# Moving weight conversions and gate products in a fused attention and channel-mixing kernel

## The chip, the cores and the metric

One core of one Trainium2 chip runs the whole program. The metric is device time in microseconds (us) of one execution. Three executions of the kernel before took 931.25 us in the median (930.16 to 931.75).

## The reference

The program computes three layers, all in float32. The first is attention with pooled queries; its output, laid out as x of shape (4, 576, 512), goes through a gated channel mixture, and that through a mixture over tokens and channels:

```
xk = mu_k * x + (1 - mu_k) * x_prev          # x_prev: x one token earlier
xr = mu_r * x + (1 - mu_r) * x_prev
k = max(xk @ w_k, 0)                         # 512 -> 1024
v = k * k @ w_v                              # 1024 -> 512
x = sigmoid(xr @ w_r) * v
theta = x @ w_theta
y = w_tok_r @ (x * cos(theta)) + w_tok_i @ (x * sin(theta))
u = x + y
out = u + max(u @ w_ch, 0)
```

The weights come as float64. The kernel turns each into a pair of float32r numbers, a high part and the rest, and every product of matrices is made of three matmuls (high by high, high by low, low by high).

## The kernel before, in words

**Stages.** Attention takes the first 427 us or so. The gated mixture follows until about 719 us, then the token mixture to the end. The gated mixture works on eight blocks of 288 tokens. Each block i needs three steps on TensorE (PE):

- `gate(i)` (L803): 48 matmuls, xr by w_r into four PSUM banks. ACT makes the sigmoid of them (L816).
- `hidden(i)` (L834): 96 matmuls, xk by w_k, eight groups f of 12. For each f ACT takes the ReLU (L836), DVE squares it (L837), ACT copies the high part (L820) and POOL subtracts for the low part (L821).
- `value(i)` (L853): 96 matmuls, the squares by w_v, eight f of 12, into four banks. At the end DVE makes four **gate products** (L858), bank by sigmoid, into the tile `XT`. They free the four banks.

PE takes them in the order gate 0, 1, 2, hidden 0, gate 3, value 0, hidden 1, gate 4, value 1, and so on, one block ahead with three gates.

**The inputs of a step.** For hidden(i) and gate(i) four input pairs x are made, one for each 128 channels: ACT scales (`xmul`, L771), DVE adds the other token (`xadd`, L776), ACT copies the high part (L782), and DVE or POOL subtracts for the low part (L783). `ahead` does this in one go for hidden(0), behind gate(1)'s matmuls.

**Ticks.** All engines read their instructions in the order in which they are written. Work beside the matmuls is hung on a counter: `tick()` is called after each f of hidden and value and after each quarter of a gate, and emits what `queue` holds for that number. Gate(1) has ticks 10 to 13, gate(2) 14 to 17, hidden(0) 18 to 25, gate(3) 26 to 29, value(0) 30 to 37, hidden(1) 38 to 45; value(5) has 126 to 133, hidden(6) 134 to 141.

**Two kinds of conversion run beside the gated mixture.**

- Five *late pieces* of w_v (k = 3 to 7, `late_v`). Their float64 words are loaded at the end of attention (L946). Each takes three ticks: first ACT's absolute value (L959) and POOL's clamp (L960); then three bit operations on DVE (L962 to L964); then ACT's high part (L967) and POOL's low part (L968). The tick of the first step is `LATE_TICK + LATE_PACE * (k - early_v)`, that is 14, 16, 18, 20, 22.
- 43 *conversion jobs* of the second mixture's weights (`conv_steps`), one every 2.7 ticks: ACT's absolute value (L127), four DVE operations (L130 to L142), ACT's copy (L146), POOL's subtraction (L150) and two stores by SP (L154, L155). The constant `SHIFT` puts all but the first load so many ticks later. The first job's DVE operations are at tick 20, the last job's at tick 133.

Loads and stores all go through SP's queue. In the second mixture `theta` (L1075) is the first user of converted weights, which SP loads with L1007.

Of the kernel before, what the change touches and what calls it, by code (L numbers as in the profile page):

```python
# [29 lines left out]
WARM = 16  # L30
THIRDS = 6
AHEAD = 3
SHIFT = 16
TURN = 4
TPOS = ((1, 0), (1, 3), (2, 0), (3, 0), (3, 3))
THETA = (1, 2, 4, 5)
# [11 lines left out]

PIECES = {"a": ((1, 2), ((2, 2), (2, 2), (2, 2)), (9, 2), 14, 15), "x": ((1, 2), ((2, 2), (2, 2), (2, 2)), (3, 2), 5, 7)}
LATE = 5  # L50
LATE_TICK = 14
LATE_PACE = 2

F64_MIN = float(np.array([0x38000000], np.uint32).view(np.float32)[0])
F64_MAX = float(np.array([0x47EFFFFF], np.uint32).view(np.float32)[0])
# [8 lines left out]
def attn_moe_kernel(ctx: ExitStack, tc: tile.TileContext, qT, kT, vP, muk, mur, wk, wv, wr, wth, wtr, wti, wch, ident, out):  # L64
# [94 lines left out]
    def attention(first):  # L159
# [491 lines left out]

        at(NT - 2, load_wr)
        follow = mixtures(WR, nat, cp)
        first_x = next(follow)
        for s, step in zip((NT - 9, NT - 7, NT - 4, NT - 2), first_x):
# [49 lines left out]
    def mixtures(WR, nat, cp):  # L705
# [9 lines left out]
        def psum():  # L715
            nb[0] += 1
            if late:
                return psum_at(LB[nb[0] % len(LB)])
            return (psm if not psn else (psm + psn))[(nb[0] - 1) % (6 if not psn else 8)]()
# [33 lines left out]
        queue = {}  # L753
# [4 lines left out]
        def tick():  # L758
            now[0] += 1
            for fn, args in queue.pop(now[0], []):  # L760
                fn(*args)
# [84 lines left out]
        def value(i, inner=()):  # L846
            b, c0 = work[i]
            k2, sg = k2s.pop(i), sgs.pop(i)
            pss = [psum()[:, :HALF] for d in range(4)]
            for f in range(8):  # L850
                for d in range(4):
                    for n, (w, c) in enumerate(PASS):
                        pe.matmul(pss[d], lhsT=WV[f][:, w, 128 * d:128 * d + 128], rhs=k2[f][:, c], start=(f == 0 and n == 0), stop=(f == 7 and n == 2))  # L853
                tick()
                if f in inner:
                    inner[f]()
            for d in range(4):
                dve.tensor_tensor(XT[b][:, d, c0:c0 + HALF], pss[d], sg[d], ALU.mult)  # L858
            if c0 and b % 2:
                pool.tensor_scalar(XT[b - 1][:, :, 576:640], XT[b][:, :, 512:576], 1.0, 1.0, op0=ALU.mult, op1=ALU.mult)  # L860

# [51 lines left out]
        for i, piece in enumerate(jobs):  # L913
            for o, f in zip((-2, 2, 3, 3, 3, 3, 4, 4, 5), conv_steps(room, piece, i, pool)):
                if o == 0 and i < 1:
                    f()
                else:
                    queue.setdefault(int(t) + o + SHIFT, []).append((f, ()))
            t += PACE
# [21 lines left out]
        early_v = 8 - LATE  # L941
# [27 lines left out]

        for k in range(early_v, 8):  # L970
            for step in range(3):
                queue.setdefault(LATE_TICK + LATE_PACE * (k - early_v) + step, []).append((late_v, (k, step)))
        order = [(gate, 0), (gate, 1), (gate, 2)]
        for i in range(8):
            order.append((hidden, i))
            if i + AHEAD < 8:
                order.append((gate, i + AHEAD))
            order.append((value, i))
# [180 lines left out]
        hidden(6)  # L1159
        theta(0)  # L1160
        value(6)
        theta(1)
        hidden(7)
        theta(2)
        value(7, {3: lambda: theta(3)})
        theta(4)
        WTK = [tile_b(8)] + [None] * 8
# [69 lines left out]
```

## Time and profile before

| | |
|---|---|
| median of three runs | 931.25 us |
| the profiled execution's own time | 932.49 us |
| its span in the trace | 930.5 us |
| PE busy | 907.8 us, 98% of the span |
| DVE, POOL, ACT busy | 74%, 64%, 58% |
| waits of PE for gate products from 500 to 760 us | 4.8 us, the longest 3.3 us |

The span covers the instructions; the execution's own time is 2 us longer. PE is almost always busy, so the places of interest are the few stretches in which it stands or runs at the lower clock. Times of single instructions are read from the trace with their start in microseconds of the span.

### The profile page before, as it was taken

Reading aid. Unit: us, or ns where it says so; the run is one execution under the profiler, and the core shown is the slowest. Engines: PE = TensorE matmul, PEld = TensorE weight load, DVE = VectorE, ACT = ScalarE, POOL = GpSimd, SP = SyncE. Lnnn points to the kernel's source line nnn. Section 1 sums busy time; section 2 is a strip of 40 time slices with the busy share of each in tenths; the row PEclk is TensorE's granted clock in tenths of the full one; section 3 lists DMA queues with packets and bytes.
Section 4 is the critical chain, followed back from the end, with each engine's and each line's share of the span. In section 5 each row is a group of like instructions: output and inputs, shape, how many; then the busy total and the mean of one; then the engine's idle time right before and its main releaser. Section 6 shows DMA issues by size and latency. Waiting matters only on the chain.

```text
span 930.5 us, 17357 instructions
## 1 busy us (share of the span) xinstructions
PE 907.8 (98%) x6292; PEld 786.4 (85%) x6292; DVE 686.7 (74%) x965; ACT 541.9 (58%) x1133; POOL 594.2 (64%) x662
## 2 busy tenths in 40 slices
PE   8999999999999999999889999998999999999998
PEld 6677777777777777768888999998999999999998
DVE  7888888888898888872699888888347663676712
ACT  8777777777777777764645565555344343443310
POOL 7877777777788777763466565666347574674631
PEclk9999999999999999999989999999899999999999
DMA  7268886777777776669323323233206200010001
GB/s 242 86 176 227 237 225 187 218 211 207 217 213 210 209 235 186 186 183 365 137 70 112 103 86 103 86 119 124 107 1 213 82 27 27 1 51 2 26 26 51
DMA packets 58773, 129.74 MB, mean 139 GB/s; under 512 B 10752, under 2 KB 29888, under 8 KB 58688
## 3 DMA queue, kind: packets, MB, share of 16 engines
q1 hardware_dynamic: 58688, 128.64, 46.4%
q8 instruction: 49, 0.80, 0.4%
q14 instruction: 36, 0.29, 0.1%
HBM read 70.46 MB, written 22.17 MB: 100 GB/s over the span
## 4 chain that ended last, share of the span: by engine, by line
PE 83%; DVE 8%; ACT 4%; issue 3%; POOL 1%; DMA 0%; SPq 0%; ACTq 0%; DVEq 0%; POOLq 0%
PE sc L303 18%; PE ty L423 16%; PE ps L1129 12%; PE ps L834 7%; PE ps L853 7%; PE ps L1148 5%; PE ps L1075 5%; PE ty L389 4%; PE tx L389 3%; PE ps L803 2%; PE sc L389 2%; DVE a L134 1%; DVE a L138 1%; ACT e L336 1%; PE ps L1033 1%
## 5 line engine op out<-in xcount | busy, mean ns | idle before, releaser
L324 DVE TENSOR_REDUCE m<-sc 128x1 f32<-128x1152 f32 x138 | 185.8, 1346 | 48.5 <-PE sc L303 47.8
L336 ACT ACTIVATE e<-sc,m 128x1152 f32<-128x1152 f32 x144 | 176.4, 1225 | 60.8 <-DVE m L324 56.2
L303 PE MATMUL sc<-kt,q 128*128 128x384 f32 (+1 forms) x864 | 192.7, 351 | 3.1 <-ACT M L400 1.7
L303 PEld LDWEIGHTS sc<-kt,q 128*128 128x128 f32 (+1 forms) x864 | 146.7, 190 | 24.4 <-issue 13.6
L834 PE MATMUL ps<-x,a 128*128 128x288 f32 x768 | 107.3, 300 | 5.8 <-DVE xt L858 4.8
L1129 PE MATMUL ps<-b,a 128*128 128x288 f32 x816 | 111.3, 296 | 0.0
L834 PEld LDWEIGHTS ps<-x,a 128*128 128x128 f32 x768 | 105.1, 193 | 6.8 <-DVE xt L858 5.5
L1129 PEld LDWEIGHTS ps<-b,a 128*128 128x128 f32 x816 | 109.4, 188 | 0.6
L853 PE MATMUL ps<-k,b 128*128 128x288 f32 x768 | 103.8, 295 | 0.1
L853 PEld LDWEIGHTS ps<-k,b 128*128 128x128 f32 x768 | 102.1, 188 | 0.6 <-ACT h L836 0.4
L202 POOL TENSOR_TENSOR kt<-kn,kh 64x576 fp32r<-64x576 f32 (+1 forms) x64 | 87.5, 1387 | 2.4
L356 DVE STREAM_TRANSPOSE blk<-e 128x1152 f32<-128x1152 f32 x60 | 81.6, 1360 | 7.4 <-ACT e L336 7.4
L423 PE MATMUL ty<-M,vn 128*64 128x320 f32 x576 | 84.4, 438 | 0.2 <-ACT M L400 0.2
L423 PEld LDWEIGHTS ty<-M,vn 128*64 128x64 f32 x576 | 38.7, 136 | 36.3 <-issue 3.8
L469 POOL TENSOR_TENSOR xt<-xt,rb 128x576 f32<-128x576 f32 x16 | 21.9, 1371 | 73.0 <-ACT xt L433 73.0
L821 POOL TENSOR_TENSOR k<-h,k 128x288 fp32r<-128x288 f32 x64 | 56.4, 897 | 18.1 <-ACT k L820 16.1
L423 PE MATMUL ty<-E,vn 128*64 128x256 f32 x540 | 64.9, 385 | 0.0
L803 PE MATMUL ps<-x,blk 128*128 128x288 f32 x384 | 56.8, 310 | 6.9 <-ACT x L782 3.5
L803 PEld LDWEIGHTS ps<-x,blk 128*128 128x128 f32 x384 | 55.1, 201 | 8.4 <-ACT x L782 4.0
L837 DVE TENSOR_TENSOR h<-h 128x288 f32<-128x288 f32 x64 | 38.5, 606 | 27.7 <-ACT h L836 27.3
L1093 ACT ACTIVATE q<-q 128x512 f32<-128x512 f32 x18 | 11.4, 632 | 79.2 <-DVE q L1090 79.2
L783 POOL TENSOR_TENSOR x<-t,x 128x288 fp32r<-128x288 f32 x52 | 44.9, 881 | 18.0 <-ACT x L782 18.0
(147 smaller groups left out, 1751.1 us busy)
## 6 DMA issues: line engine op xcount, KB each, us to landing
E<-blk SPq DMA_DIRECT2D x240, 144.0 KB
vn<-vP SPq DMA_DIRECT2D x16, 576.0 KB
kn<-kT SPq DMA_DIRECT2D x15, 576.0 KB
qn<-qT SPq DMA_DIRECT2D x15, 576.0 KB
b<-wtk SPq DMA_DIRECT2D x9, 576.0 KB
rb<-scr SPq DMA_DIRECT2D x32, 144.0 KB
out<-xt SPq DMA_DIRECT2D x32, 144.0 KB
cv<-wk SPq DMA_DIRECT2D x8, 512.0 KB
```

The costliest lines, as they stand in the source:

```text
L202: engines[e].tensor_tensor(out, x, hi.bitcast(F32), ALU.subtract)
L303: r = pe.matmul(sc[0:m, c, 0:384], lhsT=x, rhs=k[:, 384 * c:384 * c + 384], start=(i == 0), stop=(i == len(ops) - 1),)
L324: r = dve.tensor_reduce(m, scs[n][:, :, 0:384], axis=AX.XY, op=ALU.max, negate=True)
L336: r = act.activation(e, sc[:, :, 0:384], AF.Exp, bias=m, scale=1.0, accum_out=rss[P][:, t:t + 1])
L356: dve.transpose(out, es_[n].rearrange("p a b -> p (a b)").rearrange("p (k m i) -> p k m i", k=KT, m=4))
L389: r = pe.transpose(ps[:, 128 * j:128 * j + 128], flat[:, 128 * k:128 * k + 128], idn)
L423: pe.matmul(out, lhsT=vns[P][:, h, j], rhs=e, start=(x == 0), stop=(x == KT - 1))
L803: pe.matmul(pss[d], lhsT=WR[k][:, w, 128 * d:128 * d + 128], rhs=x[k][:, c], start=(k == 0 and n == 0), stop=(k == 3 and n == 2))
L821: pool.tensor_tensor(q[:, 1], h, q[:, 0].bitcast(F32), ALU.subtract)
L834: pe.matmul(ps, lhsT=WK[k, f // 4][:, w, 128 * (f % 4):128 * (f % 4) + 128], rhs=x[k][:, c], start=(k == 0 and n == 0), stop=(k == 3 and n ...
L853: pe.matmul(pss[d], lhsT=WV[f][:, w, 128 * d:128 * d + 128], rhs=k2[f][:, c], start=(f == 0 and n == 0), stop=(f == 7 and n == 2))
L1129: pe.matmul(pss[d], lhsT=zs[j][z][:, 128 * d:128 * d + 128], rhs=WTK[min(j, 8)][:, w, cs], start=(m == 0 and n == 0), stop=(m == 8 and n = ...
```

## The change

Three things are edited. The late pieces start at ticks 11, 13, 16, 19 and 22. All conversion jobs but the first load move eight ticks later. In `value` the last of the eight ticks is called behind the gate products instead of ahead of them.

```diff
-SHIFT = 16
+SHIFT = 24
...
 LATE = 5
-LATE_TICK = 14
-LATE_PACE = 2
+LATE_TICKS = (11, 13, 16, 19, 22)
...
                         pe.matmul(pss[d], lhsT=WV[f][:, w, 128 * d:128 * d + 128], rhs=k2[f][:, c], start=(f == 0 and n == 0), stop=(f == 7 and n == 2))
-                tick()
+                if f < 7:
+                    tick()
                 if f in inner:
                     inner[f]()
             for d in range(4):
                 dve.tensor_tensor(XT[b][:, d, c0:c0 + HALF], pss[d], sg[d], ALU.mult)
+            tick()
             if c0 and b % 2:
...
         for k in range(early_v, 8):
             for step in range(3):
-                queue.setdefault(LATE_TICK + LATE_PACE * (k - early_v) + step, []).append((late_v, (k, step)))
+                queue.setdefault(LATE_TICKS[k - early_v] + step, []).append((late_v, (k, step)))
```

The order of PE's instructions stays as it was. Three places on other engines, first as they stood, then as they stand. In the changed file the lines up to the gate products carry numbers lower by one, those of `late_v` and after higher by one.

ACT, between the inputs of gate(2) and the start of hidden(0)'s ReLUs. `q<-b` is a late piece's absolute value, `b<-q` its high part, `t<-xt` a scaling, `x<-t` an input's high part, `g<-ps` a sigmoid. Before:

```order
L782 CAST x_4701<-t_4633 128x288
L782 CAST x_4717<-t_4687 128x288
L771 ACTIVATE t_4732<-xt_69,mu 128x288
L771 ACTIVATE t_4734<-xt_69,mu 128x288
L771 ACTIVATE t_4736<-xt_69,mu 128x288
L771 ACTIVATE t_4738<-xt_69,mu 128x288
L782 CAST x_4744<-t_4732 128x288
L782 CAST x_4747<-t_4734 128x288
L782 CAST x_4750<-t_4736 128x288
L816 ACTIVATE g_4753<-ps 128x288 x4
L782 CAST x_4758<-t_4738 128x288
L959 ACTIVATE q_4644<-b_4650 128x512
```

Now:

```order
L781 CAST x_4701<-t_4633 128x288
L960 ACTIVATE q_4644<-b_4650 128x512
L781 CAST x_4719<-t_4687 128x288
L968 CAST b_4737<-q_4644 128x512
L960 ACTIVATE q_4644<-b_4651 128x512
L770 ACTIVATE t_4742<-xt_69,mu 128x288
L770 ACTIVATE t_4744<-xt_69,mu 128x288
L770 ACTIVATE t_4746<-xt_69,mu 128x288
L770 ACTIVATE t_4748<-xt_69,mu 128x288
L781 CAST x_4754<-t_4742 128x288
L781 CAST x_4757<-t_4744 128x288
L781 CAST x_4760<-t_4746 128x288
```

The whole of piece k = 3 and the absolute value of k = 4 have moved ahead of the four scalings of `ahead`.

DVE, in hidden(0), from the bit operations of piece k = 5 (`b_4652`) on. `h<-h` are squares, `t<-xt` the additions for gate(3)'s inputs, `a<-a` a conversion job. Before:

```order
L962 TENSOR_SCALAR q_4645<-q_4645 128x512
L963 SCALAR_TENSOR_TENSOR q_4645<-b_4652,q_4645 128x512
L964 SCALAR_TENSOR_TENSOR q_4645<-b_4652,q_4645 128x512
L776 SCALAR_TENSOR_TENSOR t_4856<-xt_70,omu,t_4856 128x288
L837 TENSOR_TENSOR h_4897<-h_4897 128x288
L130 TENSOR_SCALAR a_4791<-a_4791 128x256
L134 TENSOR_SCALAR a_4791<-a_4791 128x256
L138 SCALAR_TENSOR_TENSOR a_4791<-a_4791 128x256
L142 SCALAR_TENSOR_TENSOR a_4791<-a_4791 128x256
L776 SCALAR_TENSOR_TENSOR t_4882<-xt_70,omu,t_4882 128x288
L837 TENSOR_TENSOR h_4933<-h_4933 128x288
L962 TENSOR_SCALAR q_4645<-q_4645 128x512
```

Now:

```order
L963 TENSOR_SCALAR q_4645<-q_4645 128x512
L964 SCALAR_TENSOR_TENSOR q_4645<-b_4652,q_4645 128x512
L965 SCALAR_TENSOR_TENSOR q_4645<-b_4652,q_4645 128x512
L836 TENSOR_TENSOR h_4852<-h_4852 128x288
L836 TENSOR_TENSOR h_4873<-h_4873 128x288
L775 SCALAR_TENSOR_TENSOR t_4858<-xt_70,omu,t_4858 128x288
L836 TENSOR_TENSOR h_4897<-h_4897 128x288
L963 TENSOR_SCALAR q_4645<-q_4645 128x512
L964 SCALAR_TENSOR_TENSOR q_4645<-b_4653,q_4645 128x512
L965 SCALAR_TENSOR_TENSOR q_4645<-b_4653,q_4645 128x512
L775 SCALAR_TENSOR_TENSOR t_4882<-xt_70,omu,t_4882 128x288
L836 TENSOR_TENSOR h_4925<-h_4925 128x288
```

Piece k = 5 has moved ahead of the first two squares, and the conversion job between the additions is gone (so is a second one, further down).

DVE, at the end of value(5), with the products `xt_71<-ps`. Before:

```order
L142 SCALAR_TENSOR_TENSOR b_7281<-b_7281 128x256
L776 SCALAR_TENSOR_TENSOR t_7367<-xt_72,omu,t_7367 128x288
L130 TENSOR_SCALAR a_7340<-a_7340 128x256
L134 TENSOR_SCALAR a_7340<-a_7340 128x256
L138 SCALAR_TENSOR_TENSOR a_7340<-a_7340 128x256
L142 SCALAR_TENSOR_TENSOR a_7340<-a_7340 128x256
L858 TENSOR_TENSOR xt_71<-ps,g_6038 128x288 x4
L837 TENSOR_TENSOR h_7466<-h_7466 128x288
```

Now:

```order
L141 SCALAR_TENSOR_TENSOR b_7248<-b_7248 128x256
L775 SCALAR_TENSOR_TENSOR t_7336<-xt_72,omu,t_7336 128x288
L858 TENSOR_TENSOR xt_71<-ps,g_6005 128x288 x4
L129 TENSOR_SCALAR a_7309<-a_7309 128x256
L133 TENSOR_SCALAR a_7309<-a_7309 128x256
L137 SCALAR_TENSOR_TENSOR a_7309<-a_7309 128x256
L141 SCALAR_TENSOR_TENSOR a_7309<-a_7309 128x256
L836 TENSOR_TENSOR h_7437<-h_7437 128x288
```

The last tick's job stands behind the products. It is now the fourth job from the end; three more follow in hidden(6), where there were none.

## Rows read from the trace of the kernel before

**Rows 1.** The page, parts 1 and 4: engines' busy time, and the last chain's shares.

```profile
PE 907.8 (98%) x6292; PEld 786.4 (85%) x6292; DVE 686.7 (74%) x965; ACT 541.9 (58%) x1133; POOL 594.2 (64%) x662
...
PE 83%; DVE 8%; ACT 4%; issue 3%; POOL 1%; DMA 0%; SPq 0%; ACTq 0%; DVEq 0%; POOLq 0%
```

**Rows 2.** Busy time by stretch of 20 us; after the engines: granted clock, DMA share, GB/s.

```profile
460.00:480.00 20.00, 13.15 (x63) 12.24 (x64) 18.97 (x25) 10.11 (x25) 14.37 (x15) 0.74 0.16 53
...
500.00:520.00 20.00, 20.00 (x152) 20.00 (x152) 17.48 (x34) 11.99 (x36) 11.94 (x15) 1.00 0.34 104
640.00:660.00 20.00, 16.66 (x107) 16.43 (x106) 12.50 (x24) 7.97 (x24) 9.01 (x13) 0.83 0.57 202
```

**Rows 3.** Timeline of PE: start, length, instructions merged, [idle before and its releaser].

```profile
446.93 12.89 PE L834 MATMUL ps<-x,a 128*128 128x288 f32 x96
462.34 0.40 PE L803 MATMUL ps<-x,blk 128*128 128x288 f32 x1 [2.51 <-ACT x L782]
464.42 5.60 PE L803 MATMUL ps<-x,blk 128*128 128x288 f32 x23 [1.68 <-POOL x L783]
471.06 0.40 PE L803 MATMUL ps<-x,blk 128*128 128x288 f32 x1 [1.04 <-ACT x L782]
473.15 4.76 PE L803 MATMUL ps<-x,blk 128*128 128x288 f32 x23 [1.69 <-POOL x L783]
477.74 13.17 PE L853 MATMUL ps<-k,b 128*128 128x288 f32 x96
...
493.21 5.29 PE L834 MATMUL ps<-x,a 128*128 128x288 f32 x38 [1.00 <-POOL x L783]
499.78 6.64 PE L834 MATMUL ps<-x,a 128*128 128x288 f32 x48 [1.27 <-DVE xt L858]
...
532.04 6.64 PE L834 MATMUL ps<-x,a 128*128 128x288 f32 x48 [0.16 <-DVE xt L858]
...
633.55 12.77 PE L853 MATMUL ps<-k,b 128*128 128x288 f32 x96
646.15 1.74 PE L834 MATMUL ps<-x,a 128*128 128x288 f32 x12
651.24 7.76 PE L834 MATMUL ps<-x,a 128*128 128x288 f32 x36 [3.34 <-DVE xt L858]
```

**Rows 4.** Timeline of ACT around the start of hidden(0).

```profile
440.92 0.43 ACT L782 CAST x<-t 128x288 fp32r<-128x288 f32 x1 [0.52 <-DVE t L776]
...
442.64 1.81 ACT L771 ACTIVATE t<-xt,mu 128x288 f32<-128x288 f32 x4
...
446.85 0.69 ACT L959 ACTIVATE q<-b 128x512 f32<-128x512 f32 x1
450.23 0.62 ACT L967 CAST b<-q 128x512 fp32r<-128x512 f32 x1 [2.69 <-issue]
```

**Rows 5.** Timeline of DVE: hidden(0)'s last input, bit operations, the products of two blocks.

```profile
446.99 0.46 DVE L783 TENSOR_TENSOR x<-t,x 128x288 fp32r<-128x288 f32 x1 [0.87 <-ACT x L782]
...
448.74 0.69 DVE L963 SCALAR_TENSOR_TENSOR q<-b,q 128x512 uint32<-128x512 uint32 x1
...
458.78 1.18 DVE L963 SCALAR_TENSOR_TENSOR q<-b,q 128x512 uint32<-128x512 uint32 x1
...
499.27 1.55 DVE L858 TENSOR_TENSOR xt<-ps,g 128x288 f32<-128x288 f32 x4
...
646.28 0.52 DVE L776 SCALAR_TENSOR_TENSOR t<-xt,omu,t 128x288 f32<-128x288 f32 x1
...
650.37 1.54 DVE L858 TENSOR_TENSOR xt<-ps,g 128x288 f32<-128x288 f32 x4
```

**Rows 6.** Timeline of POOL: a late piece's low part, and gate(3)'s last input.

```profile
450.93 1.30 POOL L968 TENSOR_TENSOR b<-q,b 128x512 fp32r<-128x512 f32 x1 [2.69 <-ACT b L967]
...
474.90 1.02 POOL L783 TENSOR_TENSOR x<-t,x 128x288 fp32r<-128x288 f32 x1
```

**Rows 7.** The stretch in which the loads at the start of the mixture end.

```profile
448.00:452.00 4.00, 4.00 (x33) 4.00 (x32) 1.81 (x3) 1.77 (x5) 1.31 (x2) 1.00 0.57 208
```

## The prediction

> **What bounds the kernel now.** I read the page first. PE is busy 98% of the span and the last chain runs 83% through it [rows 1], so only a stretch in which PE stands, or runs slowly, can give time back. The table by stretch shows two: 460 to 480 us, where PE is busy 13.15 of 20 us at a mean granted clock of 0.74, and 640 to 660 us, with 16.66 us and 0.83; between them, as in 500 to 520, PE is full at clock 1.00 [rows 2]. PE's timeline then tells who is late [rows 3].
>
> - *Gate(3).* Hidden(0) ends at 446.93 + 12.89 = 459.8, and PE stands four times, 2.51 + 1.68 + 1.04 + 1.69 = 6.9 us, for ACT and POOL, which make gate(3)'s inputs. The matmuls between run at half clock: 23 in 5.60 us are 0.243 us each, against 0.131 (96 in the 12.6 us from 633.55 to 646.15), that is 1.2 instead of 2.4 GHz. Gate(3) lasts to 477.74, 17.9 us, where 48 x 0.131 = 6.3 would do.
> - *Hidden(1).* It stands 1.00 us for a POOL input and 1.27 us for the gate products; hidden(2) stands 0.16 us for its own.
> - *Hidden(6).* After one group of 12 PE stands 3.34 us for the products of value(5), and the next 36 matmuls take 7.76 us instead of 36 x 0.131 = 4.7: 3.0 us more.
>
> Why are the inputs late? DVE is busy 18.97 of the 20 us from 460 on, with 25 instructions of 0.76 us each [rows 2], and ACT and POOL, in order, stand behind it. Among these 25 are eight operations of two conversion jobs and seven of late pieces. The operations also cost more there than alone: L963 takes 1.18 us beside POOL's work, 0.69 without it [rows 5].
>
> **Term 1: gate(3).** The change takes the two jobs out and moves piece k = 5 ahead of the squares. From k = 5's first bit operation to gate(3)'s last addition DVE had 21 instructions; it keeps 12, and 9 x 0.76 = 6.8 us go. But the pieces moved forward cost something earlier, at `ahead`.
>
> ACT reaches the absolute value of piece k = 3 some 0.33 us after 440.92, at 441.3. From there to the high part takes 450.23 - 446.85 = 3.4 us, in which ACT stands, then follow 0.62 us for it and 0.69 us for the next absolute value [rows 4]. So the four scalings start at 446.0 instead of 442.64, 3.4 us later. Hidden(0)'s last input was ready at 447.45 [rows 5], and PE wanted it at 446.93 + 9 x 0.131 = 448.1: 0.7 us of slack go off. POOL's low part of k = 3 (1.30 us, [rows 6]) now runs beside the additions; I add 0.3 us. PE gets a **new wait of 3.0 us** ahead of hidden(0), which then ends at 462.8. If the clock falls behind it, hidden(0) ends later, but its squares are behind PE anyway, so I charge nothing.
>
> The chain to gate(3)'s inputs now starts so: `ahead`'s last input 3.4 + 0.6 us later, at 451.4; bit operations of k = 4, 2.0 us, to 453.4; its high part 0.6 us; from the absolute value of k = 5 to its high part 3.4 us, and POOL's low part of k = 4 in between about 0.7 us beyond that: 458.0; to POOL's start of k = 5's low part 450.93 - 450.23 = 0.7 us: 458.7. From there POOL has 13 instructions up to gate(3)'s last low part (four of late pieces, five squares, four inputs), at 14.37 / 15 = 0.96 us each [rows 2]: 12.5 us, to 471.2 if it never waits. In the old trace the last low part ended at 474.90 + 1.02 = 475.9 [rows 6]; these are the two ends. One wait for k = 6's bit operations remains in ACT's order, worth about 1.4 us, so I take **472.6**, nearer the lower end, since DVE, which held POOL up, loses a third of its queue. The last quarter of gate(3) is 12 matmuls: 1.6 us at full clock, 2.9 at half. With PE still standing before several quarters I take 2.4: gate(3) ends at 475.0 instead of 477.74. **Gain 2.7 us**, 0 to 4.9 by the two ends.
>
> The Trainium skill (SBUF — State Buffer, § SBUF: two separate sides) says that VectorE and GpSimd share one pair of ports as an exclusive lock: while one has it, the other stands for the whole instruction. By that the 12.5 us of POOL and about 5.5 us of DVE would add, the last input would come at 476.7, term 1 would be nothing and the sum 8.8 us. The row speaks against it in full: 18.97 + 14.37 = 33.3 us busy within 20 [rows 2], unless the waiting counts as busy.
>
> **Term 2: hidden(1) and (2).** Value(0)'s products came at 499.27, while PE left value(0) at 490.75, the start of the next row. In the old trace DVE entered value(0) with a backlog and three pieces or jobs still to do. From tick 28 on jobs have the same density as before (eight ticks are 2.96 jobs), so what falls away is the backlog: three jobs, at 4 x 0.76 = 3.0 us each, 9 us. The products then come at about 490.3, ahead of the fifth group of hidden(1), 6.3 us behind the end of value(0) (about 488), which wants their banks. **Gain 1.00 + 1.27 + 0.16 = 2.4 us**; nothing at the other end.
>
> **Term 3: hidden(6).** DVE ended the last addition ahead of the last tick's job at 646.28 + 0.52 = 646.8; the job stood between that and the products at 650.37 [rows 5]. Now the products go first. Two of them, at 1.54 / 4 = 0.39 us, end at 647.6; PE wants the bank of the second at 646.15 + 1.6 = 647.7 [rows 3]. The wait goes, and with it the fall of the clock: **gain 3.34 + 3.0 = 6.4 us** (at least 5, if half a microsecond of wait stays and some of the clock's loss).
>
> **What is moved and costs nothing.** Three jobs (12 DVE operations, nine on ACT and POOL, with the job before them eight stores, and one load) land in hidden(6), where DVE was busy 12.50 of 20 us, most of it ahead of 652 [rows 2]. If this cover were gone, the first `theta`'s angles would come later by one job, 3 us, with five groups of other matmuls still ahead of PE. On SP's queue the loads of theta's weights now stand behind one more load of a job and ahead of the last stores. All 4.0 MB of that stretch, at 208 / 0.57 = 365 GB/s [rows 2, 7], would take 11 us from 646.15, to 657.3; theta(0) wants them at 646.15 + 13 = 659.2. The raw words of the late pieces must have landed at 441.3: their loads were issued ahead of half of the burst that ends at 450.3 [rows 7], so I take them as landed; the other end is a wait of 9.0 us.
>
> **Sum:** 2.7 + 2.4 + 6.4 = 11.5 us. The profiled execution took 932.49, which becomes 921.0. It lies 1.2 us above the median of the runs, 931.25; that becomes **919.8 us**.
>
> **The rivals.**
>
> - *The first term is eaten* (DVE and POOL take turns, or the new wait ahead of hidden(0) is nearer 6 us than 3): sum 8.8, 922.4 us. For it: L963 at 1.18 beside POOL. The rule of the Trainium skill named above (SBUF — State Buffer) is this rival.
> - *Gate(3) runs through*: with the jobs gone all input work keeps up, and only the new 3.0 us stay. Gate(3) gives back 17.9 - 6.3 - 3.0 = 8.6, value(0) its slow start 13.17 - 12.77 = 0.4, the rest 8.8: 17.8 us, 913.5. Against it: five late pieces still stand in the same ACT queue.
> - *The early pieces wait for their words*: ACT stands to 450.3 with `ahead` behind it, and 9.0 us of the 11.5 are lost: 928.8 us. Then the change hardly does what it says.
> - *Slower: the squares become the bound.* Three values (1, 4, 5) have a job at their last tick; it now runs ahead of the squares but behind products that wait for PE, so DVE can't work it off early. If ReLU, with three `h` tiles, ran out of room, PE would stand up to 650.37 - 646.8 = 3.6 us each and lose 3.0 us of clock: 3 x 6.6 - 11.5 = 8.3 us slower, 939.6. It decides once squares lag by more than PE's free banks cover. Against it: in hidden(1) the first square came after 500.8, 8 us behind its group, and PE stood only for the products.
>
> **How the numbers follow.** Forecast 0.44, first term eaten 0.24, gate(3) through 0.16, words late 0.10, squares 0.06. A difference under 0.2%, 1.9 us, cannot be told from none; the words' case, 2.4 us, I split evenly between faster and same. Faster 0.44 + 0.24 + 0.16 + 0.05 = 0.89, same 0.05, slower 0.06. The forecast's own range is 917 to 922 (term 1 from 0 to 4.9). The 8 in 10 reach from 913, the third case, to 925, the second with term 3 at 5 and a clock that falls ahead of hidden(0); left out are the last two.
>
> **What would show it.** Right: no wait of PE for gate products over half a microsecond, 96 matmuls of hidden(6) in about 12.8 us at clock 1.00; a new wait of about 3 us ahead of hidden(0), released by ACT, DVE or POOL; gate(3) ending near 475. Wrong: a wait of hidden(0) beyond 6 us, a DMA as its releaser, a new wait of theta(0), or products still behind by more than 6 us in hidden(1).

## The result, and the profile after

The changed kernel took 919.24 us in the median of four runs (919.22 to 919.30), beside 931.49 for the kernel before on the same chip. The ratio is 0.9871, with an interval of 0.9854 to 0.9889: 12.2 us faster. The profiled execution took 919.25 us, with a span of 917.5 instead of 930.5.

Part 1 of the page, which answers to the first of [rows 1]; in part 4 PE now has 89% of the last chain.

```profile
PE 901.8 (98%) x6292; PEld 781.5 (85%) x6292; DVE 688.4 (75%) x965; ACT 542.5 (59%) x1133; POOL 597.4 (65%) x662
```

PE's waits from 425 to 760 us of the changed kernel: what it waited for, us in total, times, longest. There is none for gate products (L858) any more.

```profile
PE ps L802 <- POOL x L782: 2.9, 3, 1.9
PE ps L833 <- ACT g L815: 2.4, 1, 2.4
PE ps L802 <- ACT x L781: 0.6, 1, 0.6
```

PE's timeline of the changed kernel, which answers to [rows 3].

```profile
427.71 19.62 PE L802 MATMUL ps<-x,blk 128*128 128x288 f32 x144
449.73 14.53 PE L833 MATMUL ps<-x,a 128*128 128x288 f32 x96 [2.40 <-ACT g L815]
464.10 1.76 PE L802 MATMUL ps<-x,blk 128*128 128x288 f32 x12
466.41 0.40 PE L802 MATMUL ps<-x,blk 128*128 128x288 f32 x1 [0.56 <-ACT x L781]
468.70 1.86 PE L802 MATMUL ps<-x,blk 128*128 128x288 f32 x12 [1.89 <-POOL x L782]
471.23 1.85 PE L802 MATMUL ps<-x,blk 128*128 128x288 f32 x12 [0.67 <-POOL x L782]
473.38 1.73 PE L802 MATMUL ps<-x,blk 128*128 128x288 f32 x11 [0.30 <-POOL x L782]
474.94 12.80 PE L852 MATMUL ps<-k,b 128*128 128x288 f32 x96
487.58 12.85 PE L833 MATMUL ps<-x,a 128*128 128x288 f32 x96
500.27 6.51 PE L802 MATMUL ps<-x,blk 128*128 128x288 f32 x48
...
626.99 12.77 PE L852 MATMUL ps<-k,b 128*128 128x288 f32 x96
639.60 6.50 PE L833 MATMUL ps<-x,a 128*128 128x288 f32 x48
...
652.75 2.96 PE L1076 MATMUL ps<-blk,g 128*128 128x512 f32 x12
```

Set beside [rows 3], the starts say where the time came from. Value(0), and so the end of gate(3), comes at 474.94 instead of 477.74: 2.8 us. Value(5) starts at 626.99 instead of 633.55, 6.6 us earlier: hidden(1) and (2) and a faster value(0) added 3.8. Value(5) to the first `theta` (652.75 - 626.99 = 25.76) was 665.61 - 633.55 = 32.06 before: 6.3. With 0.1 behind it that makes the 13.0 us of the span.

Two stretches of the changed kernel, which answer to [rows 2]. After the engines: granted clock, DMA share, GB/s.

```profile
460.00:480.00 20.00, 16.59 (x120) 15.67 (x119) 17.66 (x22) 11.22 (x29) 17.12 (x17) 1.00 0.00 1
640.00:660.00 20.00, 20.00 (x145) 19.45 (x144) 14.95 (x28) 9.20 (x27) 12.30 (x15) 1.00 0.56 188
```

Three timelines of the changed kernel: ACT ahead of hidden(0), then POOL's last input of gate(3), then two blocks' gate products on DVE.

```profile
445.32 0.62 ACT L968 CAST b<-q 128x512 fp32r<-128x512 f32 x1 [2.36 <-DVE q L965]
445.85 0.66 ACT L960 ACTIVATE q<-b 128x512 f32<-128x512 f32 x1
446.42 1.80 ACT L770 ACTIVATE t<-xt,mu 128x288 f32<-128x288 f32 x4
```

```profile
472.08 1.25 POOL L782 TENSOR_TENSOR x<-t,x 128x288 fp32r<-128x288 f32 x1
```

```profile
492.72 1.54 DVE L858 TENSOR_TENSOR xt<-ps,g 128x288 f32<-128x288 f32 x4
...
639.41 1.54 DVE L858 TENSOR_TENSOR xt<-ps,g 128x288 f32<-128x288 f32 x4
```

### The profile page after: what moved, and what is told of

It reads as the page before. It is cut to its first block, busy times and chain, and to the rows that moved or that the text cites. A ratio compares the mean times of both kernels' runs of the same rounds, so it can differ in the third digit from the quotient of the medians.

```text
span 917.5 us, 17359 instructions
## 1 busy us (share of the span) xinstructions
PE 901.8 (98%) x6292; PEld 781.5 (85%) x6292; DVE 688.4 (75%) x965; ACT 542.5 (59%) x1133; POOL 597.4 (65%) x662
## 4 chain that ended last, share of the span: by engine, by line
PE 89%; ACT 4%; DVE 3%; POOL 2%; DMA 1%; issue 1%; SPq 0%; DVEq 0%; ACTq 0%; POOLq 0%
PE sc L302 17%; PE ty L422 15%; PE ps L1130 12%; PE ps L852 11%; PE ps L833 10%; PE ps L1149 6%; PE ps L1076 5%; PE ps L802 3%; PE ty L388 3%; PE tx L388 3%; PE sc L388 2%; DVE m L323 1%; ACT e L335 1%; PE ps L1034 1%; DMA rb<-scr 1%
## 5 line engine op out<-in xcount | busy, mean ns | idle before, releaser
L833 PE MATMUL ps<-x,a 128*128 128x288 f32 x768 | 105.1, 298 | 2.4 <-ACT g L815 2.4
L820 POOL TENSOR_TENSOR k<-h,k 128x288 fp32r<-128x288 f32 x64 | 59.1, 939 | 12.4 <-ACT k L819 12.1
L836 DVE TENSOR_TENSOR h<-h 128x288 f32<-128x288 f32 x64 | 42.2, 662 | 21.9 <-ACT h L835 21.2
L802 PE MATMUL ps<-x,blk 128*128 128x288 f32 x384 | 53.3, 296 | 3.4 <-POOL x L782 2.9
L399 DVE COPY M<-tx 128x512 f32<-128x512 f32 x80 | 54.5, 681 | 1.8 <-PE tx L388 1.8
```

The costliest lines, as they stand in the source:

```text
L802: pe.matmul(pss[d], lhsT=WR[k][:, w, 128 * d:128 * d + 128], rhs=x[k][:, c], start=(k == 0 and n == 0), stop=(k == 3 and n == 2))
L820: pool.tensor_tensor(q[:, 1], h, q[:, 0].bitcast(F32), ALU.subtract)
L833: pe.matmul(ps, lhsT=WK[k, f // 4][:, w, 128 * (f % 4):128 * (f % 4) + 128], rhs=x[k][:, c], start=(k == 0 and n == 0), stop=(k == 3 and n ...
```

## The experiments

Times below are medians; in brackets stand the ratio to the kernel before and its 95% interval. The kernel before stood between 931.5 and 932.3 beside them. The first series tests the prediction's picture: three separate terms, with the jobs and the late pieces both in gate(3)'s queue. "Products first" is the edit of `value`.

**One part alone.** Only products first:

```diff
-                tick()
+                if f < 7:
+                    tick()
...
+            tick()
```

> The kernel before with the gate products ahead of the last tick, ticks of late pieces and jobs as before. If the three gains stand apart, this brings term 3 alone, 6.3 us in hidden(6), and the 0.16 us of hidden(2): about 925 us. If the products' order is also what frees hidden(1), its 1.27 us go as well and the time is near 923.5. If the wait in hidden(6) came from the backlog of jobs and not from the order, it stays, and the time is above 929.

It took 925.90 us (0.9936, 0.9921 to 0.9951). The timeline of PE in this kernel: hidden(6) runs without a wait, 5.6 us are gained, and gate(3) still ends at 477.84. Hidden(1) keeps waits of 0.96 and 1.23 us; hidden(2) has none.

```profile
477.84 1.35 PE L853 MATMUL ps<-k,b 128*128 128x288 f32 x9
...
645.72 6.67 PE L834 MATMUL ps<-x,a 128*128 128x288 f32 x48
```

The changed kernel without products first:

```diff
-                if f < 7:
-                    tick()
+                tick()
...
-            tick()
```

> The changed kernel with the gate products behind the last tick again. If the gains stand apart, hidden(6) stands 3.3 us for them and runs 36 matmuls at half clock, 6.3 us more than the changed kernel: about 925.5. If shifting the jobs alone had cleared hidden(6), since other jobs stand at its start, the time stays below 921.

It took 924.46 us (0.9919, 0.9904 to 0.9934), 5.2 us above the change. Gate(3) ends at 475.00. The wait ahead of hidden(6)'s second group is back, with 2.63 us where 3.3 was expected:

```profile
644.50 5.06 PE L833 MATMUL ps<-x,a 128*128 128x288 f32 x36 [2.63 <-DVE xt L857]
```

Only the jobs' shift, on the kernel before:

```diff
-SHIFT = 16
+SHIFT = 24
```

> The kernel before with the jobs eight ticks later and nothing else. If taking the two jobs out of hidden(0) is what shortens gate(3), the gain there is at least that of the changed kernel, since the new wait of 2.4 us ahead of hidden(0) is absent: 924 to 926 us, with hidden(6) still standing 3.3 us. If the early start of the late pieces is what shortens gate(3), this gains little there and the time is near 929.

It took 925.33 us (0.9928, 0.9913 to 0.9942). PE's timeline in this kernel:

```profile
447.07 12.89 PE L834 MATMUL ps<-x,a 128*128 128x288 f32 x96
...
471.34 3.67 PE L803 MATMUL ps<-x,blk 128*128 128x288 f32 x23 [1.01 <-POOL x L783]
474.84 12.98 PE L853 MATMUL ps<-k,b 128*128 128x288 f32 x96
487.67 13.20 PE L834 MATMUL ps<-x,a 128*128 128x288 f32 x96
...
645.65 6.62 PE L834 MATMUL ps<-x,a 128*128 128x288 f32 x36 [2.63 <-DVE xt L858]
```

Gate(3) ends as early as in the whole change, with no wait ahead of hidden(0), and hidden(1) has none. So the shift alone carries term 1 and takes both waits out of hidden(1); the late pieces need not move for that. It does not carry all of term 2: hidden(2) now stands 0.85 us for its products, with a job ahead of them, and value(5) starts at 628.67, 4.9 us earlier than before, where the change gains 6.6. Another 1.9 us of its gain lie in hidden(6), whose wait is 2.63 us and not the 3.3 expected.

Only the late pieces, on the kernel before:

```diff
-LATE_TICK = 14
-LATE_PACE = 2
+LATE_TICKS = (11, 13, 16, 19, 22)
```

> The kernel before with the late pieces at ticks 11, 13, 16, 19, 22 and nothing else. If the early start is a cost by itself, hidden(0) starts 2.5 to 3 us late, the two jobs still stand between gate(3)'s additions, and the time is 931 to 934. If the early start is what shortens gate(3), the time is below 929.

It took 931.03 us (0.9992, 0.9982 to 1.0001): nothing that can be told. The wait ahead of hidden(0) comes, and gate(3) ends about where it did (0.4 us later, in a trace whose gate(0) begins 1.1 us later), since it is the end of its inputs, not hidden(0), that sets it:

```profile
450.58 14.49 PE L833 MATMUL ps<-x,a 128*128 128x288 f32 x96 [2.41 <-ACT g L815]
...
478.15 1.36 PE L852 MATMUL ps<-k,b 128*128 128x288 f32 x9
```

The change with the late pieces back at their old ticks (14, 16, 18, 20, 22):

> The changed kernel with the late pieces back at ticks 14, 16, 18, 20, 22: jobs eight ticks later and products first, but no early start. If the jobs alone shorten gate(3), it ends near 474.9 again, without the wait ahead of hidden(0), and the time is that of the changed kernel, 918.7 to 919.8 us. If the early start carries part of the gain, the time is 921 or more.

It took 919.90 us (0.9876, 0.9861 to 0.9890), 0.7 us above the change: no wait ahead of hidden(0), gate(3) ends at 474.90, and hidden(1) stands 0.18 us for the products.

The change with products first in value(5) alone:

> The changed kernel with the products ahead of the last tick in value(5) alone, behind it in the seven other values. If term 3 is one place, this costs only the wait of hidden(2) and its like, under 0.8 us, and the time is 919.2 to 920.0. If the order of the products matters in every block, the time is above 921.

It took 919.94 us (0.9876, 0.9862 to 0.9891). Only a wait of 0.42 us in hidden(2) returns: term 3 is one place.

**Can gate(3) run through?** 5.8 us of PE's standing were left (2.40 ahead of hidden(0), 3.42 in gate(3)). Five kernels move the late pieces within the change, by their ticks alone. Ticks 14, 16, 24, 26, 28:

> The changed kernel with the late pieces at ticks 14, 16, 24, 26, 28, so that no piece stands between the steps of gate(3)'s inputs. If those inputs wait for pieces in the queues of ACT, DVE and POOL, as I now hold, gate(3) follows hidden(0) with less than 2 us of waits, PE gains up to 8 us there and may lose 2 us of it in hidden(1): 911 to 915 us. If gate(3) is bound by POOL's and DVE's own work on squares and inputs, the time stays at 918 or more.

It took 920.30 us (0.9882, 0.9867 to 0.9897). PE's timeline, then ACT's, where q<-b is a piece's absolute value and b<-q its high part:

```profile
460.71 7.78 PE L802 MATMUL ps<-x,blk 128*128 128x288 f32 x48
468.32 11.50 PE L852 MATMUL ps<-k,b 128*128 128x288 f32 x84
483.74 0.53 PE L852 MATMUL ps<-k,b 128*128 128x288 f32 x2 [3.92 <-ACT b L968]
485.13 2.77 PE L852 MATMUL ps<-k,b 128*128 128x288 f32 x10 [0.86 <-POOL b L969]
```

```profile
471.55 0.62 ACT L968 CAST b<-q 128x512 fp32r<-128x512 f32 x1 [3.09 <-DVE q L965]
472.08 0.66 ACT L960 ACTIVATE q<-b 128x512 f32<-128x512 f32 x1
...
476.14 0.62 ACT L968 CAST b<-q 128x512 fp32r<-128x512 f32 x1 [2.22 <-DVE q L965]
476.67 0.68 ACT L960 ACTIVATE q<-b 128x512 f32<-128x512 f32 x1
```

Gate(3) does run through, so the pieces in its queue were what held it; but value(0) stands 4.8 us for the last piece, hidden(1) takes 14.57 us, in part at the lower clock (granted 0.83 from 480 to 500 us), and the gain is given back. On ACT each absolute value stands behind the high part of the piece before, which waits for DVE. Later still (14, 16, 24, 28, 31):

> The same with the last two pieces at ticks 28 and 31, among value(0)'s first groups. If the pieces' backlog in gate(3) and value(0) is what hidden(1) then waits for, this differs from the kernel with 26 and 28 by under 1 us, since the same work lies ahead of the products; if the last piece comes too late for value(0)'s eighth group, PE stands there, and the time is over 1 us longer.

It took 923.88 us (0.9919, 0.9902 to 0.9935): value(0) stands for two pieces, 2.08 + 0.53 and 4.16 + 0.54 us.

Then pieces that share their ticks, so that no absolute value stands behind a high part. In the next three kernels the theory is that the order of the pieces keeps gate(3) waiting, the rival that the amount of work does. Ticks 14, 16, 24, 24, 24:

> The same with ticks 14, 16, 24, 24 and 24: three pieces share their ticks behind gate(3)'s inputs, where ticks 24, 26 and 28 gave 920.3 us with value(0) standing 4.8 us for the piece k = 7. Theory (each absolute value stood behind the high part of the piece before): the wait in value(0) falls below 1.5 us, gate(3) still runs through, 914 to 917 us. Rival (amount): the same wait of 4 to 5 us in value(0), 919.5 to 921 us.

It took 919.82 us (0.9870, 0.9853 to 0.9886). The wait in value(0) fell from 4.8 to 0.19 us, as the theory says. But hidden(1) now stands 2.71 us for a sigmoid on ACT and 0.48 for an input, and runs in part at the lower clock (granted 0.74 from 480 to 500 us); the time is the rival's.

Ticks 14, 14, 15, 24, 24:

> The same with ticks 14, 14, 15, 24 and 24: no piece ahead of hidden(0)'s inputs. Theory (order, not amount): no wait ahead of hidden(0); the squares of hidden(0) start later by the three pieces' operations, which PE does not see; gate(3) below 9 us, 911 to 915 us. Rival (amount): gate(3)'s inputs or the last pieces are late by as much as the three pieces are, 918 to 921 us.

It took 919.30 us (0.9868, 0.9853 to 0.9883): gate(3) lasts 6.5 us, hidden(0) stands 3.90 us in its middle for the sigmoids that free its banks, hidden(1) 0.70 and 1.76. The time is the rival's; the theory had no wait in hidden(0).

Ticks 11, 12, 14, 24, 24:

> The changed kernel with the late pieces at ticks 11, 12, 14, 24 and 24: three pieces are finished ahead of the inputs of gate(3), two share their ticks behind them, so that no absolute value on ACT stands behind the high part of the piece before it. Theory (the pieces' order on ACT and DVE, and not the amount of work, keeps gate(3) waiting): gate(3) runs within a microsecond or two of 6.5 us, value(0) begins near 469 to 470 and stands less than 1 us for its last pieces: 912 to 915 us. Rival (the amount of work between 440 and 485 us is the limit, wherever it stands): what gate(3) gains returns as a wait ahead of hidden(0) or in value(0), 918 to 920.5 us.

It took 919.17 us (0.9863, 0.9849 to 0.9878), which the change's 919.24 can't be told from. PE's timeline in this kernel, then DVE's products of value(0):

```profile
450.45 14.52 PE L833 MATMUL ps<-x,a 128*128 128x288 f32 x96 [3.14 <-ACT g L815]
464.81 6.56 PE L802 MATMUL ps<-x,blk 128*128 128x288 f32 x48
471.21 12.86 PE L852 MATMUL ps<-k,b 128*128 128x288 f32 x96
...
486.40 5.33 PE L833 MATMUL ps<-x,a 128*128 128x288 f32 x38 [0.70 <-POOL x L782]
493.45 6.61 PE L833 MATMUL ps<-x,a 128*128 128x288 f32 x48 [1.72 <-DVE xt L858]
```

```profile
492.95 1.54 DVE L858 TENSOR_TENSOR xt<-ps,g 128x288 f32<-128x288 f32 x4
```

PE is 3.7 us ahead of the change at value(0) (471.21 against 474.94), and 0.4 us at gate(4) (499.89 against 500.27). The time is the rival's; the place, hidden(1), is one that neither had named. The products come at 492.95, in the change at 492.72: DVE's stream does not come forward when PE does. From 478 to 492 us DVE is busy 13.2 of 14 us in both, its waits behind POOL counted (last section). So DVE's queue is the next bound behind gate(3).

Last, the same with the jobs two ticks later still, `SHIFT = 26`:

> The kernel with late pieces at ticks 11, 12, 14, 24 and 24 (919.2 us), and the conversion jobs two ticks later still, SHIFT 26. With SHIFT 24 its gate(3) ran through (6.56 us), but hidden(1) stood 0.70 us for an input of POOL and 1.72 us for the products. Theory (DVE's backlog behind the late pieces is what remains, and two ticks are 0.74 of a job, 4 x 0.76 x 0.74 = 2.2 us of DVE): both waits go or nearly so, the wait of about 3 us ahead of hidden(0) stays, 916.5 to 917.5 us. Rival (the shift has reached its end): the last jobs now end too late for the loads of the second mixture's weights, PE stands ahead of the first theta or in hidden(6) and (7), 918.5 to 921 us.

It took 919.69 us (0.9870, 0.9854 to 0.9887). PE's timeline:

```profile
491.73 6.61 PE L833 MATMUL ps<-x,a 128*128 128x288 f32 x48 [1.28 <-DVE xt L858]
...
525.34 6.61 PE L833 MATMUL ps<-x,a 128*128 128x288 f32 x48 [1.67 <-DVE xt L858]
```

The time is the rival's, but none of its waits is there; the theory's is not reached either. The wait for the input went and gate(4) came at 498.18, 2.1 us earlier than in the change; but a job now stands right ahead of value(1)'s products, hidden(2) stands 1.67 us, and gate(5) starts at 531.79 against 531.95. None of the six beats the change by an amount that can be told.

## Why the prediction was right

**Term 1, predicted 2.7 us, measured 2.8.** Gate(3) ends at 474.94 where 475.0 was written. The scalings of `ahead` began at 446.42 (predicted 446.0), the wait ahead of hidden(0) was 2.40 (predicted 3.0). The prediction had PE wait for hidden(0)'s last input; it waited for ACT's sigmoids (L815), which stand behind the same scalings. The last low part ended at 472.08 + 1.25 = 473.3, 0.7 later than predicted, and the last quarter took 1.6 us where 2.4 was charged; the two errors cancel, which is luck. Hidden(0) took 14.53 us, in part at the lower clock (granted 0.91 from 440 to 460 us), and this cost nothing, since the inputs' chain set the end: without products first it took 13.38 us in the execution that was read, and gate(3) ended at 475.00 all the same.

What the step had wrong is its account of what does the work. It counted the early pieces together with the jobs. The shift alone ends gate(3) at 474.84 with no wait ahead of hidden(0), and with the old ticks of the pieces the change loses 0.7 us. So the new wait bought nothing at this place: the pieces' early start put 2.40 us of standing ahead of hidden(0) and took 1.5 us of it out of gate(3) (4.90 with the old ticks, 3.42 now). What it saved lies behind, for the most part in hidden(1), which stands 0.18 us with the old ticks and takes 13.13 us instead of 12.69.

**Term 2, predicted 2.4 us, measured 3.8.** In hidden(1) the backlog was the cause: the shift alone takes both waits out. In hidden(2) it was not, though the prediction put that wait down to it too: with the shift alone it is 0.85 us instead of 0.16, with products first alone it is gone, so there it was the order of the products. The term was sized too small, as the waits alone. Hidden(1) took 506.26 - 490.75 = 15.51 us and takes 500.27 - 487.58 = 12.69: 2.82 for waits of 2.27. Hidden(2) took 538.51 - 525.34 = 13.17 and takes 531.95 - 519.26 = 12.69: 0.48 for a wait of 0.16. So each of the three waits cost PE about 0.3 us beyond its length. Value(0) gave 0.4 more, which only the third case had counted. The products came at 492.72, not at 490.3: 1.2 us ahead of the fifth group of hidden(1), which wants them at 487.58 + 48 x 0.131 = 493.9. The margin was thin, as the runs that brought PE forward by more than that show.

**Term 3, predicted 6.4 us, measured 6.3** in the profiled executions; by medians 5.6 alone, and 5.2 when taken out of the change. It is one place, value(5). Products alone gain 5.6 us and the shift alone 6.2, together 11.7 of the 12.2, but this does not show that the terms stand apart: value(5) to the first `theta` took 32.06 us before, 30.21 with the shift alone and 25.76 in the change, so 1.9 us of the shift's gain lie in term 3's place and are not gained twice. Ahead of value(5) the whole change gains more than its parts alone, 6.6 us beside 4.9 for the shift and 0.4 for the products, and the two differences nearly cancel.

**The sum.** 11.5 us were predicted; the medians differ by 12.2, the two profiled executions by 932.49 - 919.25 = 13.2. The 1.2 us taken off for the profiled execution's place above the median made up for most of what the sum lacked. That too is luck: the changed kernel's profiled execution stands at its median, 919.25 beside 919.24.

**Rivals.** *First term eaten, and the rule of the Trainium skill (SBUF — State Buffer, § SBUF: two separate sides):* the last input came at 473.3, not at 476.7, and the new wait was 2.40 us, so term 1 was not eaten. But the rule was dismissed wrongly. DVE and POOL are busy 17.66 + 17.12 = 34.8 us within 20, and the waiting counts as busy, which is the exception that the prediction named: from 462 to 465 us the two take turns over whole instructions (last section), and there this trace agrees with the rule. What failed is the rival's sum. The 0.96 us of a POOL instruction is a mean over rows that hold such waits already (a subtraction takes 0.79 us undisturbed and 0.96 to 1.02 in gate(3) before), and 5.5 us of DVE were added to it in full. *Gate(3) runs through:* it did not. All kernels of the second series made it do so, and with ticks 11, 12, 14, 24, 24 just as this rival had it (a wait of 3.14 us ahead of hidden(0), then 6.56 us), and took 919.2 us: its 913.5 left DVE's backlog as the next bound out of account. *Words late:* ACT's first absolute value began at 441.49, with 441.3 predicted, and had not stood for a transfer. *Squares as the bound:* PE has no wait for a square from 425 to 760 us.

## What to carry to other kernels

When background work on a second engine is taken out of a stretch, look for the next thing that the engine has to deliver, and compare when it comes, not only when PE stands: here PE was brought 3.7 us forward at gate(3), and one block later waited for products that came no earlier than before. Work that nobody waits for goes behind the operation that frees PE's banks; here that cost nothing and was worth 5.2 to 5.6 of the 12.2 us. On an engine that takes its queue in order, steps of several pieces that go round over other engines hold one another up when they are written piece by piece. Interleaved (all first steps, then all second), value(0)'s wait for its last piece fell from 4.8 to 0.2 us; but hidden(1) then stood 2.71 us for ACT, and the kernel became only 0.5 us faster (919.82 beside 920.30).

## What the runs showed of the hardware that was not expected

The same wait has different prices. Without products first, hidden(6) stood 2.63 us for the products in the changed kernel and in the one with the shift alone, behind the same 12 matmuls. In one, the 36 matmuls that follow took 5.06 us, in the other 6.62; with the late pieces alone they took 6.59 behind 3.26 us, before 7.76 behind 3.34 us [rows 3]. The stretch from 640 us on of the two kernels, first without products first, then the shift alone:

```profile
640.00:650.00 10.00, 7.37 (x57) 7.14 (x56) 6.52 (x15) 4.40 (x14) 5.69 (x7) 1.00 0.70 234
```

```profile
640.00:650.00 10.00, 7.37 (x45) 7.14 (x45) 6.16 (x13) 3.64 (x10) 4.73 (x6) 0.85 0.66 215
```

PE was busy 7.37 of 10 us in both, the granted clock 1.00 in one and 0.85 in the other. The four executions without products first took 922.72, 924.30, 924.62 and 925.45 us; their mean granted clocks were 0.998, 0.996, 0.996 and 0.993, and the first is the profiled one. So the longer ones had the lower clock. That they lost it behind this wait is likely but not shown, since only one execution of each kernel has a trace; and the four of the change lie within 0.1 us with 0.996 to 0.998. What decides whether the clock falls behind such a wait stays open: the 3.0 us of clock in term 3 held for the execution that was read, and can't be counted on for another.

DVE and POOL took turns, and a profile counts the waiting as busy. Four instructions of the changed kernel that met while gate(3)'s inputs were made, then one that POOL began with DVE idle:

```profile
462.56 0.99 POOL L782 TENSOR_TENSOR x<-t,x 128x288 fp32r<-128x288 f32 x1
462.92 1.18 DVE L964 SCALAR_TENSOR_TENSOR q<-b,q 128x512 uint32<-128x512 uint32 x1
463.51 1.26 POOL L820 TENSOR_TENSOR k<-h,k 128x288 fp32r<-128x288 f32 x1
464.13 1.19 DVE L965 SCALAR_TENSOR_TENSOR q<-b,q 128x512 uint32<-128x512 uint32 x1
...
470.39 0.79 POOL L782 TENSOR_TENSOR x<-t,x 128x288 fp32r<-128x288 f32 x1
```

The four end at 463.55, 464.10, 464.77 and 465.32, so 0.55, 0.67 and 0.55 us apart: each ends its own undisturbed length (0.69 us for a bit operation, as in [rows 5], 0.79 for a subtraction), less 0.12 to 0.14, behind the end of the other engine's instruction. The 1.18 us are thus a wait for POOL and 0.69 us of work, and busy times of the two that add to more than the span do not show that they worked at the same time.
